# Reordering the opening of a four-layer kernel: row 0 centred before its scale is known, row 1's statistics on ScalarE, the mask pattern stored ahead of the norms

## Chip, cores, metric

One core of a Trainium2 chip runs the whole program. The metric is the device time of one execution in microseconds; the kernel before takes 1152.85 us (median of three runs, 1152.61 to 1153.31). Inputs and outputs are bf16, sums are fp32.

## What is computed

Four layers in the order A, B, A, B, each with a residual: x = x + layer(layernorm(x)). S = 2048 rows, D = 576 columns.

```
def _A_ref(x, wqkv, wo):                 # 32 heads of 18, window 8, dilation 2
    q, k, v = split(x @ wqkv)
    idx = pos[:, None] - 2 * arange(8)[None, :]
    logits = einsum('bhsd,bhswd->bhsw', q, k[idx]) * scale   # -1e9 where idx < 0
    o = einsum('bhsw,bhswd->bhsd', softmax(logits), v[idx])
    return o @ wo

def _B_ref(x, w_in, w_sp, b_sp, w_out):  # gMLP
    z = gelu(x @ w_in); z1, z2 = halves(z)
    g = w_sp @ layernorm(z2) + b_sp
    return (z1 * g) @ w_out
```

Only the opening of the first layer A is changed. What matters of it: layernorm of the input rows, the product of the normalised rows with the v, k and q parts of wqkv, and the mask of the attention window.

## The kernel before

Rows are handled in 16 blocks of 128 ("rows 0" is the first block; even and odd positions are split into the two halves of the sequence, so that a dilation of 2 becomes a window over neighbours). `xnT` holds the normalised rows transposed, 128 x 5 x 2048, and feeds every product on TensorE. Layer A writes v into `v_ext` (17 overlapping tiles of keys, 19 columns for each head, of which the last is 1 and gives the softmax sum), and q and k into `QK`. In `QK` each head takes 32 partitions: 18 of data, 14 "window rows" that hold a mask pattern, so that the product of q and k carries the mask with it.

The opening is written out by hand, in program order on each of the five engines: an instruction waits for its operands and holds everything behind it on its own engine.

- `x_load` fetches row blocks: 0, 1, 2 to 3 apart, then 4 to 7 (into `x1`), 8 to 11 (into the spare part of `oT`), 12 to 15 (`x3`, into the buffer of rows 0 to 3). `load_wv` fetches the v weights, `load_wqk` the q and k weights in six transfers. Nearly all go through SP's queue, one after another.
- 46 matmuls on an identity (line 699) run before there is data; `zero_right` clears the unused halves of three weight tiles on VectorE.
- `build_window_rows` makes the mask pattern and returns four parts. `part0` computes bit patterns on VectorE, `pads` clears the tile `win_pat` on GpSimd, `part1` finishes the pattern in `oT` on VectorE (lines 166 to 173) and stores it to DRAM by two transfers, `part2` makes the pattern of the first eight columns on GpSimd and stores it. `load_pat` fetches the pattern back into `win_pat` by four transfers, spread over partitions. `fill_window_rows` copies it into `QK`: for each half of the head groups (`g0`) one copy for each side (q, k) and a small one of the first columns.
- The layernorm of a block i: `B_` (two bn_stats, line 715), `G_` (bn_aggr, 718), `R_` (add epsilon on VectorE, line 727, then the power -1/2 on GpSimd, 728), `A_` (subtract the mean, times the scale, line 735, into one of four `xn_bufs`). Blocks 0 to 3 are transposed on TensorE (`T_pe`, line 742) and copied by ScalarE into `xnT` (745); blocks 4 to 15 by a transposing transfer on SP's queue (`T_`, line 306).
- `VW(t, hh)` is the product of key tile t with half of the v weights: five matmuls (line 451) into a PSUM bank, evacuated into `v_ext`. Key tile t begins at row 120 t; tile 1 needs the last eight columns of block 0 beside block 1.
- `PG(d, qk, cc)` is the product for q and k: weight block d, 512 columns cc of `xnT`, five matmuls (line 462), evacuated by ScalarE into a staging tile; when a staging tile is full, four or five transfers for each d move the heads into `QK`, by turns on GpSimd's and SP's queues. cc = 0 needs blocks 0 to 3, cc = 1 blocks 4 to 7. After the eighteen units of cc 0 and 1 come `VW` 4 to 7, then cc = 2 and the attention steps.
- Line 703 writes the ones column of `v_ext` on ScalarE; `setup_bufs` clears the pads of the attention's buffers on GpSimd.

PSUM tiles come from a ring of five banks; a tile waits until the bank's former content has been read.

Of the kernel before, what the change touches and what calls it, by code (L numbers as in the profile page):

```python
# [18 lines left out]
P = 128  # L19
# [44 lines left out]
class K:  # L64
# [53 lines left out]
    def build_window_rows(self, c, R):  # L118
# [43 lines left out]
        def pads():  # L162
            nc.gpsimd.memset(pat[:], 0.0)

        def part1(eng):
            nc.vector.tensor_scalar(out=vf[:], in0=bits[:], scalar1=-2.0, scalar2=1.0, op0=ALU.mult, op1=ALU.add)
            Rf = R[:].rearrange("p a r b m -> p a r (b m)")
            nc.vector.tensor_scalar_mul(out=Rf[:, :, 0:8, :], in0=Rf[:, :, 0:8, :], scalar1=vf[:, 4, 1:2])
# [28 lines left out]
    def fill_window_rows(self, QK, half):  # L197
        nc, n = self.nc, self.cfg.S // 2
        for g0 in (0, 4):
            for a in range(2):  # L200
                nc.vector.tensor_copy(out=QK[:, a, g0:g0 + 4, half * n:(half + 1) * n].rearrange("p g (k x) -> p g k x", x=P),
                                      in_=self.pat[:, a, half, None, None, :].to_broadcast([P, 4, n // P, P]))
            if half == 0:
                nc.vector.tensor_copy(out=QK[:, :, g0:g0 + 4, 0:8], in_=self.pat0[:, :, None, :].to_broadcast([P, 2, 4, 8]))
# [176 lines left out]
    def layer_A(self, li):  # L381
# [65 lines left out]
        def VW(t, hh, dve):  # L447
            nk = tdim(t)[0]
            pv = self.PT_tile([P, 512], f32, "pv")
            for c in range(5):  # L450
                nc.tensor.matmul(pv[:nk, 0:288], lhsT=self.xnT[:, c, k0_(t):k0_(t) + nk],  # L451
                                 rhs=wv_sb[:, c, hh * 288:(hh + 1) * 288], start=(c == 0), stop=(c == 4))
            evac(v_ext[:nk, t, 16 * hh:16 * hh + 16, 0:DH], pv[:nk, 0:288].rearrange("p (b d) -> p b d", d=DH), dve)
# [222 lines left out]
        if li == 0:  # L676
# [26 lines left out]
            nc.scalar.copy(out=v_ext[:, :, :, DH:DH + 1], in_=self.ones[:, None, None, :].to_broadcast([P, NT, H, 1]))  # L703
            rows[0]()
            rows[1]()
            setup_bufs(nc.gpsimd)
# [17 lines left out]

            def R_(i0, n):
                rs = rstds[:, i0:i0 + n]
                nc.vector.tensor_scalar_add(out=rs, in0=mvs[:, i0:i0 + n, 1], scalar1=EPS)
                nc.gpsimd.tensor_tensor(out=rs, in0=rs, in1=self.neg_half[:, 0:1].to_broadcast([P, n]), op=ALU.pow)
# [9 lines left out]
            def T_pe(i):  # L738
                xn = xns.pop(i)
# [3 lines left out]
                r = i * P  # L743
                for c0, c1 in ((0, 3), (3, 5)) if i == 0 else ((0, 5),):
                    nc.scalar.copy(out=self.xnT[:, c0:c1, r:r + P], in_=pt[:, c0:c1])  # L745
# [523 lines left out]
```

## Time and profile before

| | |
|---|---|
| median of three runs | 1152.85 us (1152.61 to 1153.31) |
| the profiled execution | 1152.74 us |
| its span, from the first to the last instruction | 1150.9 us |
| TensorE busy in the span | 1142.6 us, 99% |
| VectorE, ScalarE, GpSimd busy | 539.7, 370.5, 259.6 us |
| granted TensorE clock, mean | 1.000 |

How to read the views: a line of the timeline gives the start in us from the span's start, the time, the engine, the source line, the operation, the tiles written and read, a count where equal instructions are merged, and in brackets the idle time of the engine before it and what ended it. An engine with a q (SPq, POOLq) is its sequencer: for a transfer the row is the time to issue it, not to move it. The chain of waits follows the last instruction back, at each step to what released it.

### The profile page before, as it was taken

What the parts mean: (1) busy time and instruction counts of PE and PEld (TensorE: products, weight loads), DVE (VectorE), ACT (ScalarE), POOL (GpSimd) and SP (SyncE); (2) the same over time, 40 slices, a digit from 0 to 9 for tenths busy, and PEclk for the clock granted to TensorE, in tenths of its full rate; (3) what the DMA queues carried; (4) which work ended last, traced back from release to release, by engine and by line L of the source; (5) the groups of instructions that cost most, each with busy time, mean ns of one, the idle gap of its engine ahead of it and who ended that gap; (6) DMA issues with size and microseconds to landing.
All of it is one profiled execution on the core that took longest, in us unless ns stands there. A gap on an engine that the chain in (4) does not pass through costs nothing.

```text
span 1150.9 us, 29693 instructions
## 1 busy us (share of the span) xinstructions
PE 1142.6 (99%) x12930; PEld 614.5 (53%) x12949; DVE 539.7 (47%) x1198; ACT 370.5 (32%) x660; POOL 259.6 (23%) x387
## 2 busy tenths in 40 slices
PE   8999999999999999999999999999999999999998
PEld 5567554444444444457755775544444444444676
DVE  8789987312233222244466889843322223222312
ACT  5589565011111111102247876541111111011000
POOL 3689654000000000002153767530000000000000
PEclk9999999999999999999999999999999999999999
DMA  8877696000000000049455867920000000001322
GB/s 195 183 164 200 141 211 137 10 13 13 13 1 13 13 13 2 1 152 213 110 110 110 180 152 176 246 60 1 13 13 13 13 13 1 13 2 30 101 74 58
DMA packets 177372, 91.26 MB, mean 79 GB/s; under 512 B 128788, under 2 KB 170420, under 8 KB 177242
## 3 DMA queue, kind: packets, MB, share of 16 engines
q1 hardware_dynamic: 164762, 70.75, 28.1%
q0 software_dynamic: 5888, 12.72, 4.6%
q10 hardware_dynamic: 6592, 5.90, 1.7%
q8 instruction: 101, 1.65, 0.6%
q14 instruction: 29, 0.24, 0.1%
HBM read 35.46 MB, written 14.69 MB: 44 GB/s over the span
## 4 chain that ended last, share of the span: by engine, by line
PE 97%; ACT 1%; DVE 1%; issue 0%; DVEq 0%; ACTq 0%
PE hh L234 79%; PE pp L462 6%; PE pv L451 3%; PE pw L629 3%; PE O_ps L559 3%; PE L_ps L536 2%; ACT P_sb L545 1%; PE L_ps L462 1%; PE hh L1191 0%; PE pt L595 0%; DVE ln_st L715 0%; DVE ln_xn L735 0%; DVE win_bits L158 0%; ACT v_ext L445 0%; ACT xnT L745 0%
## 5 line engine op out<-in xcount | busy, mean ns | idle before, releaser
L234 PE MATMUL hh<-Wq,Z 64*128 64x512 bf16 x4608 | 505.8, 376 | 0.0
L234 PEld LDWEIGHTS <-Z 64*128 64x128 bf16 x6984 | 339.8, 94 | 310.1
L1095 DVE TENSOR_TENSOR g_tmp<-hh,ln_xn 128x512 f32<-128x512 f32 x144 | 92.8, 686 | 452.3 <-PE hh L234 452.3
L947 ACT COPY bank_turn<-ones 1x1 bf16<-1x1 bf16 x239 | 44.8, 188 | 538.5 <-PE hh L234 538.5
L78 POOL DMA_DIRECT2D wout<-in_B_w_out_dram x4 | 4.3, 1075 | 602.0 <-PE hh L234 602.0
L234 PE MATMUL hh<-wout,Z 64*128 64x288 bf16 x2232 | 137.0, 283 | 0.0
L545 ACT ACTIVATE P_sb<-L_ps 128x1440 bf16<-128x1440 f32 (+3 forms) x136 | 125.0, 971 | 24.6 <-PE L_ps L536 23.2
L234 PE MATMUL hh<-xnT,w 64*128 64x512 bf16 x1152 | 132.2, 376 | 0.0
L234 PE MATMUL hh<-win2a,xnT 64*128 64x512 bf16 (+1 forms) x960 | 118.7, 355 | 0.0
L234 PEld LDWEIGHTS <-xnT 64*128 64x128 bf16 x1440 | 69.9, 94 | 70.0 <-issue 0.5
L1020 DVE BATCH_NORM_STATS2 z_st<-zp 128x6 f32<-128x512 bf16 (+1 forms) x160 | 93.0, 624 | 13.0 <-ACT zp L1018 12.9
L1086 ACT ACTIVATE z1T<-hh 128x1024 bf16<-128x1024 f32 x72 | 73.7, 1024 | 61.9 <-PE hh L234 61.9
L234 PEld LDWEIGHTS <-w 64*128 64x128 bf16 x1152 | 56.1, 94 | 68.3
L1096 DVE TENSOR_TENSOR Z<-g_tmp,z1T 128x512 bf16<-128x512 f32 x144 | 92.4, 683 | 0.0
L1018 ACT ACTIVATE zp<-hh 128x1024 bf16<-128x1024 f32 (+1 forms) x96 | 76.1, 810 | 48.8 <-PE hh L234 48.6
L462 PE MATMUL pp<-xnT,wqk_sb 128*128 128x512 bf16 (+1 forms) x313 | 74.2, 379 | 0.9
L234 PE MATMUL hh<-win2b,xnT 64*128 64x512 bf16 (+1 forms) x480 | 72.8, 355 | 0.0
L1160 DVE TENSOR_TENSOR x_new<-hh,xo 128x288 bf16<-128x288 f32 x64 | 26.3, 453 | 93.0 <-PE hh L234 85.0
L299 POOL TENSOR_SCALAR ln_xn<-x_new,ln_mv,ln_rstd 128x576 bf16<-128x576 bf16 x28 | 64.2, 2293 | 2.7
L78 POOL DMA_DIRECT2D QK<-stg x76 | 48.0, 636 | 36.5 <-DVE stg L443 21.9
L462 PEld LDWEIGHTS <-wqk_sb 128*128 128x128 bf16 (+1 forms) x360 | 32.1, 97 | 36.6 <-issue 1.9
L1044 POOL TENSOR_SCALAR Z<-zp,z_mv,z_rstd 128x256 bf16<-128x256 bf16 x32 | 50.7, 1584 | 3.5
(124 smaller groups left out, 753.3 us busy)
## 6 DMA issues: line engine op xcount, KB each, us to landing
xres<-x_new SPq DMA_DIRECT2D x44, 144.0 KB
wout<-in_B_w_out_dram POOLq DMA_DIRECT2D x4, 1296.0 KB, 7.4
xo<-xres SPq DMA_DIRECT2D x32, 144.0 KB
xn_rows<-ln_xn SPq DMA_DIRECT2D x28, 160.0 KB
w<-in_B_w_in_dram SPq DMA_DIRECT2D x16, 256.0 KB
QK<-stg POOLq DMA_DIRECT2D x51, 72.0 KB, 4.4
QK<-stg SPq DMA_DIRECT2D x37, 72.0 KB
xo<-in_A_x_dram SPq DMA_DIRECT2D x6, 288.0 KB
```

Source lines behind the costliest of these rows:

```text
L78: return eng.dma_start(out=out, in_=in_)
L234: ins = self.nc.tensor.matmul(outs[a_], lhsT=lhs(a_, c, r0), rhs=rhs(a_, c, r0), start=start and k_ == 0, stop=stop and k_ == len(chunks) ...
L299: e.tensor_scalar(out=xn[:nrows, 0:D], in0=x_t[:nrows, :], scalar1=mv[:nrows, 0:1], scalar2=rstd[:nrows, 0:1], op0=ALU.subtract, op1=ALU.mult)
L462: nc.tensor.matmul(pp, lhsT=w, rhs=self.xnT[r0:r1, c, cc * 512:(cc + 1) * 512], start=start, stop=stop, tile_position=(r0, 0))
L545: nc.scalar.activation(out=P_bufs[2 * jp + s % 2][:nk, :, :, 0:nq], in_=Lv[:nk, :, :, 0:nq], func=ACT.Exp, scale=scale)
L947: self.turn_on = lambda tok: nc.scalar.copy(out=tok, in_=self.ones[0:1, 0:1])
L1018: nc.scalar.activation(out=zp[:, w0:w0 + n], in_=pz, func=ACT.Gelu_apprx_tanh)
L1020: nc.vector.bn_stats(out=st[:, x // 512, :], in_=zp[:, x:x + min(512, w0 + n - x)])
L1044: eng.tensor_scalar(out=Z[:, b0:b1, i, :], in0=zv[:, b0:b1, :], scalar1=mv[:, 0:1], scalar2=rstd[:, 0:1], op0=ALU.subtract, op1=ALU.mult)
L1086: lambda ht, z1T=z1T, q2=q2: nc.scalar.activation(out=z1T[:, q2 * 512:(q2 + 2) * 512], in_=ht[:].rearrange("p a b -> p (a b)"), func=ACT.G ...
L1095: nc.vector.tensor_tensor(out=tmp[:], in0=pg[:, a_, :], in1=bsp[:, qs], op=ALU.add)
L1096: nc.vector.tensor_tensor(out=uT(jj)[:, sub, qs], in0=tmp[:], in1=z1Ts[jj, sub][:, qs], op=ALU.mult)
```

## The change

- Order on SP's queue: the stores of the pattern go behind the load of rows 4 to 7 and ahead of the six loads of the q and k weights; the four loads of the pattern follow these, then rows 8 to 11. Rows 12 to 15 are loaded after the transposes of blocks 4 to 7.
- VectorE: `win_pat` is cleared here; two of the three weight clears go to GpSimd, later; `part1` runs right behind `part0`, ahead of all statistics, with its largest multiplication on GpSimd (line 168). `part2` follows at once, and its store is issued by SP.
- Row block 0: after its mean it is centred without the scale, transposed (`xcT`, in an `o_slot`) and used for `VW(0, 0)` and `VW(0, 1)`; the scale is applied as ScalarE evacuates the product (`scaled`). Block 0 is then normalised and transposed a second time for `xnT`, in two copies (the last eight columns first).
- Row block 1: sum and sum of squares on ScalarE (Identity and Square with an accumulator), mean and scale on GpSimd.
- 35 identity matmuls in place of 46. The ones column of `v_ext` is written in four quarters between the evacuations of the first `PG` units. `setup_bufs` goes behind the scales of blocks 0 to 3.
- `fill_window_rows` is cut in pieces: the first half of the groups between the statistics of block 7 and the normalisation of blocks 6 and 7, the second half around the normalisation of blocks 8 to 11.

```diff
-            nc.gpsimd.memset(pat[:], 0.0)
+            nc.vector.memset(pat[:], 0.0)
...
-            nc.vector.tensor_scalar_mul(out=Rf[:, :, 0:8, :], in0=Rf[:, :, 0:8, :], scalar1=vf[:, 4, 1:2])
+            nc.gpsimd.tensor_scalar(out=Rf[:, :, 0:8, :], in0=Rf[:, :, 0:8, :], scalar1=vf[:, 4, 1:2], scalar2=None,
+                                    op0=ALU.mult)
...
-            x_load(x1[:, 0:4, :], 4, 4, nc.sync)
-            self.load_wqk(nc.sync)
-            x_load(spare, 8, 4, nc.sync)
             exp_table()
-            self.zero_right()
...
-            for _ in range(46):
+            for _ in range(35):
...
-            nc.scalar.copy(out=v_ext[:, :, :, DH:DH + 1], in_=self.ones[:, None, None, :].to_broadcast([P, NT, H, 1]))
+            x_load(x1[:, 0:4, :], 4, 4, nc.sync)
+            rows[1]()
+            nc.vector.memset(wv_sb[64:128, 4, :], 0.0)
             rows[0]()
-            rows[1]()
-            setup_bufs(nc.gpsimd)
+            rows[2](nc.sync)
+            rows[3](nc.sync)
+            self.load_wqk(nc.sync)
+            self.load_pat(nc.sync)
+            x_load(spare, 8, 4, nc.sync)
...
+            def scaled(out, in_):
+                nc.scalar.activation(out=out, in_=in_, func=ACT.Identity, scale=rstds[:, 0:1])
+            sums = sb.tile([P, 2], f32, name="lnx_sum", tag="lnx_sum", bufs=1)
+            spill = self.xn_bufs[1][:, 0:D]
+            nc.scalar.activation(out=spill, in_=xts[1], func=ACT.Identity, accum_out=sums[:, 0:1])
+            nc.gpsimd.tensor_scalar(out=mvs[:, 1, 0:1], in0=sums[:, 0:1], scalar1=1.0 / D, scalar2=None, op0=ALU.mult)
+            nc.scalar.activation(out=spill, in_=xts[1], func=ACT.Square, scale=-1.0, bias=mvs[:, 1, 0:1],
+                                 accum_out=sums[:, 1:2])
             S_(0)
-            R_(0, 1)
-            for i in range(3):
-                B_(i + 1)
-                A_(i)
-                G_(i + 1)
-                R_(i + 1, 1)
-                T_pe(i)
-                for t, hh in (((0, 0),), ((0, 1),), ((1, 0), (1, 1)))[i]:
-                    VW(t, hh, False)
-            rows[2](nc.sync)
+            E_(0, 1)
+            xc = self.xn_bufs[0]
+            nc.vector.tensor_scalar(out=xc[:, 0:D], in0=xts[0], scalar1=mvs[:, 0, 0:1], scalar2=None, op0=ALU.subtract)
+            W_(0, 1)
+            B_(2)
+            pt = T_mm(xc)
+            xcT = o_slots[0]
+            for c0, c1 in ((0, 3), (3, 5)):
+                nc.scalar.copy(out=xcT[:, c0:c1], in_=pt[:, c0:c1])
+            scaled(*VW_mm(0, 0, xcT))
+            A_(0)
+            nc.gpsimd.tensor_scalar(out=rstds[:, 1:2], in0=sums[:, 1:2], scalar1=1.0 / D, scalar2=EPS,
+                                    op0=ALU.mult, op1=ALU.add)
+            W_(1, 1)
+            G_(2)
+            E_(2, 1)
+            A_(1)
+            W_(2, 1)
+            pt0 = T_mm(xns.pop(0))
+            T_out(0, pt0, r0=P - 8)
+            pt = T_mm(xns.pop(1))
+            T_out(1, pt)
+            v01 = VW_mm(0, 1, xcT)
+            scaled(*v01)
+            T_out(0, pt0, r1=P - 8)
+            B_(3)
+            G_(3)
+            E_(3, 1)
+            A_(2)
+            W_(3, 1)
             A_(3)
+            nc.gpsimd.memset(wqk4[64:128, :], 0.0)
+            v0 = VW_mm(1, 0)
+            pt = T_mm(xns.pop(2))
+            T_out(2, pt)
+            evac(*v0, False)
+            v1 = VW_mm(1, 1)
+            pt = T_mm(xns.pop(3))
+            T_out(3, pt)
+            evac(*v1, False)
             VW(2, 0, False)
...
+            setup_bufs(nc.gpsimd)
+            nc.gpsimd.memset(wo_sb[64:128, 4, :], 0.0)
+            S_(4, 5)
+            R_(4, 2)
+            S_(6)
+            A_(4, 5)
+            T_(4, 5)
+            S_(7)
+            R_(6, 2)
+            self.fill_window_rows(QK, 0, (0,))
+            A_(6, 7)
+            T_(6, 7)
             x3 = sb.tile([P, 4, D], bf16, name="x_in3", tag="x_in", bufs=2)
...
-            S_(4, 5)
-            R_(4, 2)
-            A_(4, 5)
-            T_(4, 5)
-            S_(6, 7)
-            R_(6, 2)
-            rows[3](nc.gpsimd)
-            A_(6, 7)
-            T_(6, 7)
-            S_(8)
-            self.load_pat(nc.sync)
-            S_(9, 10, 11)
+            S_(8, 9, 10, 11)
             R_(8, 4)
-            S_(12)
-            A_(8, 9, 10, 11)
-            T_(8, 9, 10, 11)
-            self.fill_window_rows(QK, 0)
-            S_(13, 14, 15)
...
+                if k_ < 4:
+                    hs = slice(8 * k_, 8 * k_ + 8)
+                    nc.scalar.copy(out=v_ext[:, :, hs, DH:DH + 1],
+                                   in_=self.ones[:, None, None, :].to_broadcast([P, NT, 8, 1]))
+                if k_ == 1:
+                    self.fill_window_rows(QK, 0, (4,), (0,))
+                    A_(8, 9, 10, 11)
+                    T_(8, 9, 10, 11)
+                    self.fill_window_rows(QK, 0, (4,), (1,))
+                    S_(12, 13, 14, 15)
```

`T_mm` holds the five transposes of the former `T_pe`, `T_out` its copy on ScalarE; `E_` and `W_` are the two halves of `R_`; `VW_mm` is `VW` without the evacuation.

More of the change, by code (lines that the diff above doesn't have):

```diff
@@ L450, in VW @@
             for c in range(5):
-                nc.tensor.matmul(pv[:nk, 0:288], lhsT=self.xnT[:, c, k0_(t):k0_(t) + nk],
+                nc.tensor.matmul(pv[:nk, 0:288], lhsT=self.xnT[:, c, k0_(t):k0_(t) + nk] if xT is None else xT[:, c, 0:nk],
                                  rhs=wv_sb[:, c, hh * 288:(hh + 1) * 288], start=(c == 0), stop=(c == 4))
-            evac(v_ext[:nk, t, 16 * hh:16 * hh + 16, 0:DH], pv[:nk, 0:288].rearrange("p (b d) -> p b d", d=DH), dve)
+            return v_ext[:nk, t, 16 * hh:16 * hh + 16, 0:DH], pv[:nk, 0:288].rearrange("p (b d) -> p b d", d=DH)
+        def VW(t, hh, dve):
+            evac(*VW_mm(t, hh), dve)
         stg_tiles, stg_left = {}, {}
@@ L742, in T_pe, with T_out @@
                     nc.tensor.transpose(pt[:, c, :], xn[:, c * P:(c + 1) * P], self.ident[:])
-                r = i * P
-                for c0, c1 in ((0, 3), (3, 5)) if i == 0 else ((0, 5),):
-                    nc.scalar.copy(out=self.xnT[:, c0:c1, r:r + P], in_=pt[:, c0:c1])
+                return pt
+            def T_out(i, pt, c0=0, c1=5, r0=0, r1=P):
+                nc.scalar.copy(out=self.xnT[:, c0:c1, i * P + r0:i * P + r1], in_=pt[:, c0:c1, r0:r1])
             def T_(*tiles):
```

24 lines of the change are left out of this document (13 added, 11 removed).

## The prediction

> **What bounds the kernel now.** I read the page's busy times first, then its chain of waits, then that chain and TensorE's waits for the opening alone, then the timeline of the first 30 us.
>
> ```profile
> PE 1142.6 (99%) x12930; PEld 614.5 (53%) x12949; DVE 539.7 (47%) x1198; ACT 370.5 (32%) x660; POOL 259.6 (23%) x387
> ...
> PE 97%; ACT 1%; DVE 1%; issue 0%; DVEq 0%; ACTq 0%
> ```
>
> TensorE sets the time: 1142.6 of 1150.9 us. An edit off TensorE counts only where TensorE waits, so the places where it waits have to be found. The chain of the opening, and TensorE's waits and busy time behind it:
>
> ```profile
> 8.81 0.45 PE pt L742 x5
> ...
> 13.85 10.74 PE pp L462 x49
> ```
>
> ```profile
> PE L_ps L536 <- ACT P_sb L545: 0.2, 1, 0.2
> ```
>
> ```profile
> 13.40:33.00 19.60, 19.50 (x92) 8.91 (x92) 17.47 (x47) 10.38 (x19) 8.03 (x14) 1.00 0.74 141
> 48.00:121.00 73.00, 71.88 (x1422) 50.99 (x1426) 62.86 (x189) 63.59 (x76) 60.59 (x78) 1.00 0.77 184
> ```
>
> Up to 8.81 us the chain runs over VectorE; from there it is TensorE. From 13.42, where the q and k products begin, to 60 us the only wait is 0.2 us on ScalarE; of 13.4 to 33.0 us TensorE is idle for 0.10, of 48 to 121 for 1.12. Nothing that the change moves behind 13.42 us can give back more than these tenths, but it can take. The question is when "pp" (line 462) starts, and whether it then runs without a stop. The steps ahead of it:
>
> ```profile
> 1.10 0.54 DVE L340 MEMSET wqk_sb<- 64x576 uint32 x1 [0.18 <-issue]
> ...
> 1.95 0.30 DVE L342 MEMSET wo_sb<- 64x288 uint32 x1
> ...
> 2.28 0.17 DVE L154 TENSOR_SCALAR win_n<-win_n 128x3 int32<-128x3 int32 x1
> ...
> 3.00 0.98 DVE L158 TENSOR_SCALAR win_bits<-win_g 128x3 int32<-128x3 int32 x4
> ...
> 3.06 0.40 POOL L151 MEMSET ln_xn<- 128x64 bf16 x4
> 3.28 0.70 DVE L160 TENSOR_SCALAR win_bits<-win_n 128x3 int32<-128x3 int32 x1
> 3.39 0.54 POOL L163 MEMSET win_pat<- 128x528 bf16 x1
> 3.56 0.82 DVE L715 BATCH_NORM_STATS2 ln_st<-x_in 128x6 f32<-128x288 bf16 x2
> ...
> 4.42 0.21 DVE L718 BATCH_NORM_AGGREGATE lnx_mv<-ln_st 128x2 f32<-128x12 f32 x1
> ...
> 4.66 0.15 DVE L727 TENSOR_SCALAR lnx_rstd<-lnx_mv 128x1 f32<-128x1 f32 x1
> 4.73 0.81 DVE L715 BATCH_NORM_STATS2 ln_st<-x_in 128x6 f32<-128x288 bf16 x2
> ...
> 5.51 0.43 DVE L735 TENSOR_SCALAR ln_xn<-x_in,lnx_mv,lnx_rstd 128x576 bf16<-128x576 bf16 x1
> ...
> 6.00 0.45 PE L742 MATMUL pt<-ident,ln_xn 128*128 128x128 bf16 x5 [0.65 <-DVE ln_xn L735]
> ...
> 6.49 0.75 ACT L745 COPY xnT<-pt 128x384 bf16<-128x384 bf16 x2 [1.38 <-PE pt L742]
> ...
> 7.03 0.79 PE L451 MATMUL pv<-wv_sb,xnT 128*128 128x288 bf16 x5 [0.57 <-ACT xnT L745]
> ...
> 7.65 0.44 PE L742 MATMUL pt<-ident,ln_xn 128*128 128x128 bf16 x5
> ...
> 7.93 0.78 PE L451 MATMUL pv<-wv_sb,xnT 128*128 128x288 bf16 x5
> ```
>
> From row 0's statistics at s = 3.56 to its transposes at 6.00 take 2.44 us; the first copy on ScalarE, call it a, starts at 6.49 = s + 2.93; pp starts at a + 6.93.
>
> **Row 0 centred first.** bn_stats to bn_aggr 0.86 (3.56 to 4.42), to epsilon 0.24, to the next VectorE instruction 0.07, the centring 0.43 (as line 735), to TensorE 0.06 (5.94 to 6.00): 1.66 in place of 2.44. The first copy then starts at a = s + 1.66 + 0.49 = s + 2.15, a gain of 0.78 us if s stays. It costs a second transposition of row 0 on TensorE: 0.28 us (7.65 to 7.93). A v product takes 0.62 (7.03 to 7.65). TensorE has 8 x 0.62 + 4 x 0.28 = 6.08 us behind the first copy, against 8 x 0.62 + 3 x 0.28 = 5.80; before, the other 1.13 of its 6.93 went to waiting for copies.
>
> I walked ScalarE and TensorE through the new order with intervals from the same stretch (a 128x640 copy 0.60 to the next start, a v evacuation 0.30, the scaled one 0.38 as an estimate). Row 1's copy ends at a + 2.63, so VW(1, 0) starts at a + 2.67 after a wait of 0.33; row 2's copy ends at a + 4.48, just ahead of VW(2, 0); pp starts at a + 7.0. So the second transposition eats what less waiting gives: +0.07 us. VectorE is ahead on this walk: A_(1) at s + 2.95 ends 0.15 before TensorE wants it, A_(2) 0.5.
>
> **The mask pattern ahead of the norms** moves s. Two clears leave VectorE (0.54 and 0.30) and one of about 0.28 enters (264 words, between lines 342 and 340): part0 starts at 1.72 instead of 2.28. But part1 now stands ahead of the statistics:
>
> ```profile
> 8.97 0.16 DVE L166 TENSOR_SCALAR win_vf<-win_bits 128x15 f32<-128x15 int32 x1
> ...
> 9.17 0.28 DVE L168 TENSOR_SCALAR oT<-oT,win_vf 128x256 bf16<-128x256 bf16 x1
> ...
> 9.80 0.25 DVE L173 TENSOR_SCALAR oT<-win_uu 128x4 bf16<-128x4 f32 x2
> ...
> 9.95 0.42 DVE L735 TENSOR_SCALAR ln_xn<-x_in,lnx_mv,lnx_rstd 128x576 bf16<-128x576 bf16 x1
> ```
>
> From line 166 to the next statistic this is 0.98, less 0.21 for line 168: 0.77 us. And it must wait for the bits. These were issued at 3.00 to 3.28 and all ended at 3.98, when GpSimd's run of memsets (line 151, then 163, to 3.93) had ended. Without line 163 that run ends at 3.46, so line 166 starts between 2.98 (bits done as early as they are issued) and 3.50, and s lies at 3.75 or at 4.27 if nothing else interferes. Line 168 on GpSimd is not shown; its nearest rows:
>
> ```profile
> L299 POOL TENSOR_SCALAR ln_xn<-x_new,ln_mv,ln_rstd 128x576 bf16<-128x576 bf16 x28 | 64.2, 2293 | 2.7
> ...
> L179 POOL COPY win_first<-oT 1x224 bf16<-1x224 bf16 x1 | 0.4, 361 | 0.0
> ```
>
> By the copy it takes 0.4 us, by the two-operation scaling 1.0 (256/576 of 2.29), at most 1.6 (halfway from there to the whole 2.29); the copy is nearer, a single pass, and I take 0.6. If VectorE's lines 171 to 173 finish only when it does, as the bits did, s is 3.65 + 0.6 + 0.23 = 4.5, at worst 5.5. I take s = 4.4: row 0's statistics start 0.84 later than now. Then a = 6.55 (6.49 before) and pp starts at 13.55 (13.42 before). The bounds are s = 3.75, pp at 12.9, and s = 5.5, pp at 14.65; row 0's landing, no later than 3.56, gives 12.7 as the floor.
>
> [...]
>
> **Row 1 on ScalarE.** Identity and Square on 576 columns, each at most as long as this row:
>
> ```profile
> L293 ACT ACTIVATE ln_xn<-x_new,ln_nmr,ln_rstd 128x576 bf16<-128x576 bf16 x15 | 13.0, 868 | 62.3 <-POOL bank_turn L1130 59.0 <-POOL ln_nmr L283 3.3
> ```
>
> ScalarE is idle from 2.68 on, as the ones column moves away. But Square waits for a mean from GpSimd, behind line 168 and part2 (an estimate of 0.7: the copy of 0.36, a small one and two memsets; the mean itself 0.25): ready at 3.65 + 0.6 + 0.7 + 0.25 = 5.2, Square ends near 6.0, ahead of a = 6.55. With line 168 at 1.6 us it ends at 7.0, still ahead of that case's a = 7.65. Cost nothing; each 0.1 us beyond is 0.1 us of a.
>
> **Queues.** The two stores, and a third, are put on SP's queue ahead of the q and k weights:
>
> ```profile
> 2.58 2.53 ACT L703 COPY v_ext<-ones 128x544 bf16<-128x544 bf16 x1
> ...
> 4.59 4.50 SPq L78 DMA_DIRECT2D wqk_sb<-in_A_wqkv_dram  x6
> ...
> 10.16 2.24 SPq L78 DMA_DIRECT2D win_period<-oT  x2
> ...
> 14.03 6.20 SPq L306 DMA_TRANSPOSE xnT<-ln_xn  x4
> ...
> 21.81 1.60 SPq L78 DMA_DIRECT2D win_pat<-win_period  x4
> ...
> 24.71 2.36 DVE L201 COPY QK<-win_pat 128x4096 bf16<-128x4096 bf16 x2 [0.39 <-DMA win_pat<-win_period]
> ```
>
> ```profile
> 2.00:4.00 2.00, 2.00 (x22) 2.00 (x20) 1.86 (x11) 1.99 (x3) 1.87 (x16) 1.00 0.96 300
> ```
>
> The weights are issued from about 6.8 instead of 4.59 (stores from 4.6, 2.2 us) to 11.3. From 2 us on the DMA engines are full at 300 GB/s, and rows 0 to 7 with the v weights (1.84 MB) keep them so to about 8.1 us; the weights of the first two pp units (1.25 MB) take 4.2 us from there: 12.3, with 0.5 for the small packets 12.8. They are needed at 13.55 and 14.6. Cost nothing; 0.7 us of slack.
>
> Rows 4 to 7 are needed nine units of 5 x 0.216 us behind the start of pp, at 23.3. VectorE ends A_(3) at 9.65; the statistics of four blocks at 1.0 (3.56 to 4.66 less 0.1 of overlap) and A_(4, 5), 0.7: 14.4. The pattern's four loads, 1.6 us behind the weights, are issued to 12.9 and there by then; two mask copies 2.5: 16.9; A_(6) 0.45; the last two transposes are issued to 20.2, where the four ended before (14.03 + 6.20). Cost nothing; cover: the nine units, some 2 us.
>
> The ones column, four quarters of about 0.7 us, lies in ScalarE's gaps (TensorE gives it 1.08 us for each evacuation of 0.59, and five banks). Starting the moves into QK three microseconds sooner meets no waiting TensorE: worth at most the 0.2 us of the waits above; I count 0.
>
> **The sum.** +0.06 (first copy) + 0.07 (to pp) = +0.13 us on 1152.74, the profiled execution, which stands 0.11 below the median: 1152.9 us.
>
> **Rivals.**
> - *Everything closes.* s = 3.75 (-0.52) or row 0's landing (-0.7), and the later waits go too, since QK is filled sooner: -0.3 to 33 us and around 50, -1.1 up to 121. 1150.6 us at best, 1152 for a third of it; beyond 0.2% only with waits that modelled matmul ends hide. For it: VectorE and GpSimd are idler there. Against it: those waits are on ScalarE's exponentials, which are not touched.
> - *The mask gates rows 4 to 7* (slower). A_(6, 7) now stand behind two copies that wait for the pattern, three transfers deep: stores, weights, loads. It decides once the pattern lands after about 16.5 us; each microsecond later is one of TensorE idle at 23.3. If the loads wait behind the 1.33 MB of weights and rows 8 to 11 as well, landing is near 19: +2.7 us, 1155.5. For it: before, the copies at 24.71 waited for the same transfer, which was issued only at 21.8. Against it: rows 8 to 11 are issued behind it.
> - *TensorE falls back to its slow pace* (slower). 35 warming matmuls end near 4.7, and until 7.1 there is only one transposition.
>
> ```profile
> 1.40:3.80 2.40, 2.40 (x24) 1.00 0.81 237
> 4.20:5.30 1.10, 1.10 (x21) 1.00 1.09 321
> ```
>
> Early identity matmuls come every 100 ns, late ones every 52, though the clock column says 1.00 for both. If the 6.1 us of transposes and v products ran at the slow pace, they would cost up to +6; for half of it +3: 1155.9. It decides from 2.2 us of extra time. Against it: gaps of 0.65 and 0.57 us did nothing before; the new ones are about 1.4 and 0.6. [...]
> - *The change doesn't do what it says*: Square holds the first copy, as priced above; at most +0.5, inside the forecast.
>
> **Chances.** A measurement of this kernel can tell about 0.2% (2.3 us) from no change. Forecast 0.62 (its own range 1152.0 to 1154.0, the bounds of s), everything closes 0.14 (over 0.2% in 0.08), the mask 0.13 (0.10), the pace 0.11 (0.08). Faster 0.08, same 0.74, slower 0.18. The range 1151.0 to 1155.6 leaves out the far halves of three rivals.
>
> **What would show it.** Right: row 0's bn_stats near 4.4, its first ScalarE copy near 6.5, pp at 13.4 to 13.7, no TensorE wait from there to 33 us. [...] A time outside 1150.4 to 1155.2 would mean a wait that I have not seen.

## The result, and the profile after

| | before | after |
|---|---|---|
| median (six runs of each, side by side) | 1153.03 us (1152.61 to 1153.31) | 1158.37 us (1157.67 to 1161.14) |
| ratio | 1 | 1.0050 (95% interval 1.0037 to 1.0063) |
| the profiled execution, its span | 1152.74, 1150.9 us | 1157.67, 1155.9 us |

The change costs 5.3 us, 0.5%. The page of the changed kernel, its busy times and its chain of waits:

```profile
PE 1146.1 (99%) x12943; PEld 615.9 (53%) x12943; DVE 539.8 (47%) x1193; ACT 372.3 (32%) x669; POOL 262.2 (23%) x390
...
PE 97%; ACT 1%; DMA 1%; DVE 1%; issue 0%; POOL 0%; SPq 0%; DVEq 0%; ACTq 0%
```

TensorE is busy 3.5 us longer (1142.6 before), 1.6 of them ahead of the first q and k product (12.17 against 10.54), so part of the loss is slower work, not waiting; and the chain now has 1% on DMA, which it did not have. TensorE's waits from 13.4 to 62 us (line, releaser: us in total, times, longest):

```profile
PE L_ps L540 <- DMA QK<-stg: 1.6, 3, 0.8
PE pp L466 <- DMA xnT<-ln_xn: 0.8, 1, 0.8
```

They have no counterpart before, where the one wait behind 13.4 us was 0.2 us on ScalarE. Where each stands, in TensorE's timeline:

```profile
44.38 0.23 PE L540 MATMUL L_ps<-QK 32*128 32x128 bf16 x3 [0.51 <-DMA QK<-stg]
45.43 0.23 PE L540 MATMUL L_ps<-QK 32*128 32x128 bf16 x3 [0.82 <-DMA QK<-stg]
45.94 0.23 PE L540 MATMUL L_ps<-QK 32*128 32x128 bf16 x2 [0.28 <-DMA QK<-stg]
...
55.39 1.24 PE L466 MATMUL pp<-xnT,wqk_sb 128*128 128x512 bf16 x5 [0.75 <-DMA xnT<-ln_xn]
```

Matmul by matmul against the trace of before, the delay builds up so: +1.43 us at the first q and k product (13.42 to 14.85), +3.60 at the first product with v (48.48 to 52.08; the logits before it arrive in four groups instead of together, which is more than their 1.6 us of waits), +4.38 behind the wait at 55 us, +4.72 at the end of the first feed-forward layer (580.72 to 585.44), +4.57 at the last product, +5.00 at the last instruction. Four places, then: the opening, the attention's start, 0.34 us in the first feed-forward layer, 0.43 us after the last product.

**The opening.** Timeline of the changed kernel:

```profile
3.93 0.96 POOL L168 TENSOR_SCALAR oT<-oT,win_vf 128x256 bf16<-128x256 bf16 x1 [0.43 <-DVE win_uu L170]
...
4.43 0.80 DVE L720 BATCH_NORM_STATS2 ln_st<-x_in 128x6 f32<-128x288 bf16 x2
...
6.02 0.77 ACT L768 ACTIVATE ln_xn<-x_in,lnx_mv 128x576 bf16<-128x576 bf16 x1 [1.40 <-POOL lnx_mv L767]
6.70 0.18 ACT L768 ACTIVATION_READ_ACCUMULATOR ln_xn<-x_in,lnx_mv 128x1 f32 x1
6.79 0.73 ACT L779 COPY o_slot<-pt 128x384 bf16<-128x384 bf16 x2
...
10.35 1.24 DVE L746 TENSOR_SCALAR ln_xn<-x_in,lnx_mv,lnx_rstd 128x576 bf16<-128x576 bf16 x1 [0.44 <-POOL lnx_rstd L735]
10.38 1.05 POOL L802 MEMSET wqk_sb<- 64x1152 bf16 x1
```

Row 0's statistics begin at 4.43. The Square of row 1 waits 1.40 us for its mean, and the first copy can only follow it at 6.79. Row 3's normalisation takes 1.24 us instead of 0.43 while GpSimd's memset runs. The identity matmuls (us, PE busy and their count) and the chain from the first product on:

```profile
1.40:5.40 4.00, 3.88 (x35) 1.00 0.90 258
```

```profile
7.30 1.38 PE pv L452 x5
8.68 1.07 PE pt L752 x10
...
15.01 19.43 PE pp L466 x90
```

All 35 identity matmuls came 0.11 us apart, where before the last 21 came 0.05 apart. From the first v product (five matmuls) to the next start on TensorE the timeline has 1.18 us (7.30 to 8.48) and for the ten transposes behind it 1.06, where before these were 0.62 and 0.56 (the chain counts a piece until the matmul's end, 1.38 and 1.07): TensorE ran at half pace through the first products. The record of the granted clock begins at 9.98 us here and at 4.01 before; ahead of its record the clock column of a view says 1.00, whatever the pace, so "the pace rises" is read below from the start of the record and from the spacing of the matmuls.

**The attention's start.** VectorE and SP's queue in the kernel before:

```profile
17.67 0.81 DVE L715 BATCH_NORM_STATS2 ln_st<-oT 128x6 f32<-128x288 bf16 x2
```

```profile
23.51 5.17 SPq L306 DMA_TRANSPOSE xnT<-ln_xn  x4
28.79 7.71 SPq L78 DMA_DIRECT2D QK<-stg  x9
```

SP's queue in the changed kernel, and VectorE and GpSimd ahead of it:

```profile
6.85 5.06 SPq L78 DMA_DIRECT2D wqk_sb<-in_A_wqkv_dram  x6
12.02 2.27 SPq L78 DMA_DIRECT2D win_pat<-win_period  x4
15.78 0.40 SPq L78 DMA_DIRECT2D oT<-in_A_x_dram  x1
16.27 6.82 SPq L307 DMA_TRANSPOSE xnT<-ln_xn  x4
...
27.32 6.16 SPq L307 DMA_TRANSPOSE xnT<-ln_xn  x4
33.58 7.69 SPq L78 DMA_DIRECT2D QK<-stg  x9
```

```profile
17.22 2.36 DVE L202 COPY QK<-win_pat 128x4096 bf16<-128x4096 bf16 x2 [0.70 <-DMA win_pat<-win_period]
...
20.80 0.81 DVE L720 BATCH_NORM_STATS2 ln_st<-oT 128x6 f32<-128x288 bf16 x2
...
24.92 1.92 POOL L735 TENSOR_TENSOR lnx_rstd<-lnx_rstd,neg_half 128x4 f32<-128x4 f32 x1 [7.62 <-DVE lnx_rstd L731]
...
26.87 1.45 DVE L746 TENSOR_SCALAR ln_xn<-oT,lnx_mv,lnx_rstd 128x576 bf16<-128x576 bf16 x4 [0.90 <-POOL lnx_rstd L735]
```

Rows 8 to 11 are loaded from 15.78, their statistics begin at 20.80 (17.67 before), their transposes are issued from 27.32 (23.51 before), and the seventeen moves into `QK` that share SP's queue start behind them, at 33.58 instead of 28.79. The chain of waits names that as the path, with the wait at 55 us behind it:

```profile
40.49 7.15 DMA QK<-stg
...
52.62 2.63 DMA xnT<-ln_xn
```

**The two small losses.** In the first feed-forward layer ScalarE now waits 0.9 us for TensorE ahead of its table load, where before it loaded at once and waited behind it. At the end SP waits 1.5 us for the last store in one piece (before: 1.1 in two), with seven of the other transfers' semaphores still to be read behind it, which takes 0.43 us (1154.53 to 1154.96), where before the last store's was the last one read:

```profile
ACT L1072 <- PE hh L235: 0.9, 1, 0.9
```

```profile
SPq L1318 <- DMA out_dram<-x_new: 1.5, 1, 1.5
```

### The profile page after: what moved, and what is told of

It is laid out like the page before. It is cut to its first block, busy times and chain, and to the rows that moved or that the text cites. A ratio compares the mean times of both kernels' runs of the same rounds, so it can differ in the third digit from the quotient of the medians.

```text
span 1155.9 us, 29716 instructions
## 1 busy us (share of the span) xinstructions
PE 1146.1 (99%) x12943; PEld 615.9 (53%) x12943; DVE 539.8 (47%) x1193; ACT 372.3 (32%) x669; POOL 262.2 (23%) x390
## 4 chain that ended last, share of the span: by engine, by line
PE 97%; ACT 1%; DMA 1%; DVE 1%; issue 0%; POOL 0%; SPq 0%; DVEq 0%; ACTq 0%
PE hh L235 79%; PE pp L466 5%; PE pv L452 4%; PE pw L633 3%; PE O_ps L563 3%; PE L_ps L540 2%; DMA QK<-stg 1%; PE L_ps L466 1%; ACT P_sb L549 1%; PE hh L1245 0%; DVE QK L202 0%; PE pt L599 0%; DMA xnT<-ln_xn 0%; PE pt L752 0%; ACT L1072 0%
```

## The experiments

Each kernel ran beside the kernel before, whose median was 1153.34 us for the first four, 1152.94 for the next four, then 1152.93 for three, 1152.85, and 1152.94 for the last two. The intervals of the ratios reach 1.0 to 1.5 us to either side, so a difference of 1 us between two changed kernels rests on their traces more than on their times. Theory: the loss is two separate things, the slow pace of the opening and the late blocks 8 to 11.

**46 identity matmuls again, alone** (`range(35)` to `range(46)`).

> The changed kernel with 46 warming matmuls again in place of 35. Theory (the loss is the sum of two: TensorE's slow pace to 10 us, some 1.1 us, and the blocks 8 to 11 that come late for the moves into QK, some 3 us): with 46 the pace rises before the first transposes, the q and k products start at 13.6 (13.3 to 13.9) instead of 14.85, TensorE still waits for the moves at 43 to 46 us and for the transposes at 54 us, and the time is 1.0 to 1.4 us below the changed kernel, about 1157.1. Rival (the pace is not set by the number of warming matmuls, or the products wait for the copies anyway): the start stays at 14.5 or later, as 11 more matmuls at 107 ns end at 6.4 and hold the transposes, and the time is that of the changed kernel or up to 0.6 more.

Measured 1160.38 us, ratio 1.0058 (1.0045 to 1.0071): no gain. The pace rose in time (record from 5.52) and the products started at 14.23, yet TensorE lost it all, and more, to waits for data:

```profile
PE pp L466 <- DMA xnT<-ln_xn: 1.6, 1, 1.6
...
PE pp L466 <- DMA wqk_sb<-in_A_wqkv_dram: 1.1, 1, 1.1
```

Behind the wait of 1.6 us the clock itself was lower. The same execution in two windows (TensorE's busy time is the second number, PEclk the third from the end):

```profile
53.32:56.71 3.39, 1.85 (x37) 0.98 (x35) 2.10 (x5) 2.94 (x4) 1.28 (x3) 1.00 0.92 108
56.73:60.12 3.39, 3.31 (x38) 1.47 (x39) 0.69 (x1) 0.40 (x1) 2.27 (x5) 0.50 1.00 300
```

Behind a stretch in which TensorE was busy 1.85 of 3.39 us the clock is 0.50 for 3.41 us; from 60.14 it is 1.00 again.

**The kernel before with 35** (`range(46)` to `range(35)`).

> The kernel before with 35 warming matmuls in place of 46, nothing else. Theory: fewer of them let the pace rise late here too, the q and k products start at 14.2 to 15 instead of 13.42, the time is 0.7 to 1.5 us above before (1153.7 to 1154.5), and the runs spread wider. Rival (the long gap between warming and the second product is what keeps the pace low, not the count): the pace rises near 4.0 us as before and the time is within 0.3 us of before.

Measured 1153.99 against 1153.34, ratio 1.0003 (0.9994 to 1.0012), runs from 1152.44 to 1155.91. The profiled one (1154.18) had the pace up only at 10.56 and its products from 14.98. So the pace can come late there too. The medians differ by 0.65 us, which the interval does not tell from none; what the other runs did is not seen.

**Mask copies back behind the transposes of blocks 8 to 11, alone; then with 46 matmuls.**

```diff
-            self.fill_window_rows(QK, 0, (0,))
             A_(6, 7)
...
-                    self.fill_window_rows(QK, 0, (4,), (0,))
                     A_(8, 9, 10, 11)
                     T_(8, 9, 10, 11)
-                    self.fill_window_rows(QK, 0, (4,), (1,))
+                    self.fill_window_rows(QK, 0)
```

> The changed kernel with all mask copies put behind the transposes of rows 8 to 11, where they stood before; 35 warming matmuls as changed. Theory: the transposes of rows 8 to 11 are issued from 23.5 to 24.5 instead of 27.3, SP's moves into QK start 3 us sooner, TensorE's waits of 1.6 us at 43 to 46 and 0.75 us at 54 shrink to under 0.5 together; the products still start at 14.85; the time is 2.0 to 2.9 us below the changed kernel, 1155.5 to 1156.4. Rival (the late pattern, the weights' place on the queue or the pow on GpSimd make them late): the transposes are issued at 26.5 or later, and the time is within 0.6 us of the changed kernel.

> Both edits together: 46 warming matmuls, mask copies behind the transposes of rows 8 to 11. Theory of two separate losses: the savings add up, 3.2 to 4.2 us below the changed kernel, 1154.2 to 1155.2; products from 13.6, no wait of TensorE over 0.5 us from 13.6 to 60. Rival (one loss covers the other): the saving is that of the larger one alone, under 3 us.

Measured 1156.75 (1.0031, 1.0021 to 1.0041) and 1156.60 (1.0023, 1.0014 to 1.0033): by the medians about 1.6 us of the 5.3 come from the place of the mask copies, less than expected, and the matmuls add nothing on top. The transposes of blocks 8 to 11 came at 26.50 and 26.78, hardly sooner. The timeline of the second run has the reason:

```profile
16.25 0.40 SPq L78 DMA_DIRECT2D oT<-in_A_x_dram  x1
...
21.15 0.82 DVE L720 BATCH_NORM_STATS2 ln_st<-oT 128x6 f32<-128x288 bf16 x2 [3.08 <-DMA oT<-in_A_x_dram]
```

With the copies gone VectorE stands idle: x rows 8 to 11 are issued only behind the weights and the pattern. In the changed kernel the copies hid this wait. The first of the two runs also shows the clock falling in the opening, to 11.40 us, after 1.49 us of work in 3.39:

```profile
4.58:7.97 3.39, 1.49 (x17) 1.03 (x15) 2.74 (x11) 1.50 (x4) 2.74 (x10) 1.00 1.01 281
7.99:11.39 3.40, 3.40 (x22) 2.52 (x20) 2.89 (x7) 2.28 (x5) 2.10 (x3) 0.50 1.01 107
```

**SP's queue in the earlier order, on top of the last run; and alone.**

```diff
-            rows[2](nc.sync)
-            rows[3](nc.sync)
             self.load_wqk(nc.sync)
-            self.load_pat(nc.sync)
             x_load(spare, 8, 4, nc.sync)
+            rows[2](nc.sync)
+            rows[3](nc.sync)
+            self.load_pat(nc.sync)
```

> The kernel with 46 warming matmuls and the mask copies behind the transposes of rows 8 to 11, and in addition SP's queue in the earlier order: q and k weights, x rows 8 to 11, then the pattern's stores and loads. In the run without this last edit VectorE stood idle for 3.08 us ahead of the statistics of row 8 (21.15), since the load of x rows 8 to 11 was issued only at 16.25. Theory now (that load, behind the pattern's stores and loads, is the second thing that makes the blocks 8 to 11 late, and hid behind the mask copies in the changed kernel): statistics of row 8 at 17.8 to 18.5, transposes of rows 8 to 11 from 23.5 to 24.3, no wait of 0.67 us in the second q and k product and none of 0.9 us at 50 us; the time is 1.8 to 2.6 us below that run's 1156.6, so 1154.0 to 1154.8. Rival (something else holds them, the rows' own statistics or SP's transposes): statistics of row 8 later than 20, time within 0.6 of 1156.6.

> The changed kernel with nothing but SP's queue in the earlier order (weights, x rows 8 to 11, then the pattern's stores and loads); 35 warming matmuls and the mask copies ahead of rows 6 and 7 as changed. Theory (either cause alone makes blocks 8 to 11 late): the statistics of row 8 still begin behind the mask copies, at 20.5 or later, the transposes of rows 8 to 11 from 26.5 or later, and the time is within 0.7 us of the changed kernel's 1158.4. Rival (the queue was the cause all along): transposes from 24.5 or sooner and 1.8 to 2.6 us saved.

On top: 1155.62 (1.0024, 1.0015 to 1.0033), 1.0 us less by the medians, not 1.8 to 2.6; 0.4 of it lies in the kernel before that ran beside each, and the two ratios (1.0023 and 1.0024) show no gain. The trace shows why. The statistics of row 8 began at 17.85 and the waits for weights and moves went, as expected; but a new stop of 1.44 us came at 24.1. The profile puts it down to an evacuation that was done 0.8 us before the stop's end; what was late are the transposes of blocks 4 to 7, behind the pattern's loads, which wait for its stores:

```profile
12.60 0.92 SPq L78 DMA_DIRECT2D win_period<-win_first  x1
16.67 2.04 SPq L78 DMA_DIRECT2D win_pat<-win_period  x4
18.81 5.28 SPq L307 DMA_TRANSPOSE xnT<-ln_xn  x4
```

Alone: 1160.67 (1.0067, 1.0054 to 1.0080), 2.3 us worse than the change as it is, where at most 0.7 was expected. The mask copies stayed ahead of blocks 6 and 7, and with the pattern issued later they gated them:

```profile
19.95 2.36 DVE L202 COPY QK<-win_pat 128x4096 bf16<-128x4096 bf16 x2 [3.57 <-DMA win_pat<-win_period]
```

TensorE's records show a stop of 3.1 us at 24.1. (The pace was up in this execution: record from 5.44, products at 14.24, with the same 35 identity matmuls and the same opening on TensorE as the changed kernel's 9.98 and 14.85.) So the two moves of the change depend on each other: early copies need an early pattern, and the early pattern holds the load of rows 8 to 11.

**TensorE's gap filled; the memset later.** Both on top of the run with 1155.62.

```diff
             pt = T_mm(xc)
+            for _ in range(8):
+                nc.tensor.matmul(warm[:, 0:P], lhsT=self.ident[:], rhs=self.ident[:], start=True, stop=True)
```

```diff
-            nc.gpsimd.memset(wqk4[64:128, :], 0.0)
...
             setup_bufs(nc.gpsimd)
+            nc.gpsimd.memset(wqk4[64:128, :], 0.0)
```

> As the run with 46 warming matmuls, late mask copies and the earlier queue order, with 8 more warming matmuls put between row 0's first transposes and its first product, where TensorE stands idle for 0.66 to 1.0 us. The clock record changes only at the ends of windows of 3.41 us; with TensorE busy for 0.78 of one it rose once and stayed low once, with 0.55 or less it fell. Theory (the pace follows the busy share of such a window, whose place against the kernel's start differs from run to run): with the gap filled the pace rises by 7 us and does not fall, the runs spread by under 1.5 us, and the median lies 0 to 0.6 us below the run without the filling. Rival (the pace is set by the warming block alone): no difference in spread, and up to 0.4 us more, as the matmuls hold the first product.

> As the run with 46 warming matmuls, late mask copies and the earlier queue order, with GpSimd's memset of the weights' last rows (1.05 us from 10.35) put behind its other memsets. It ran beside row 3's normalisation on VectorE, which took 1.24 us instead of 0.43. Theory (the two share a path to memory): row 3's normalisation takes 0.45, its transposes start 0.26 us sooner, and the products start 0.2 to 0.4 us sooner; time 0.2 to 0.4 us lower. Rival (the transposes wait for a copy anyway): normalisation short, start of the products as in the run without it, within 0.1.

Measured 1155.75 (1.0026, 1.0015 to 1.0036) and 1155.64 (1.0024, 1.0015 to 1.0033): no difference. The filled gap tells nothing apart, as the runs without it were close together too, but for one. With the memset later, row 3's normalisation took 0.84 us (other memsets now ran beside it) and the products started at 13.99 instead of 14.23; the stop at 24 us grew from 1.44 to 1.84 in return. What the two engines share was a guess of the theory that no run shows; shown are the scaling's 1.24 us beside the one memset and its 0.84 beside the others. The gain was real and was taken back by the late transposes.

**The pattern's loads behind the transposes of blocks 4 to 7**, on top of the later memset (`self.load_pat(nc.sync)` moved ahead of `S_(8, 9, 10, 11)`).

> The run with 46 warming matmuls, late mask copies, earlier queue order and later memset, and now the pattern's four loads behind the transposes of rows 4 to 7 on SP's queue. In that run the loads waited 2.4 us for the pattern's stores and held these transposes (first at 18.97), so that TensorE stopped for 1.84 us at 23.9. Theory: the first transposes are issued by 15.5, no wait of TensorE over 0.3 us from the start of the q and k products (13.9 to 14.0) to 60 us, and the time falls by 1.4 to 1.8 us to 1153.8 to 1154.3; what is left against before is the later start (0.5), 0.3 in the second layer and 0.4 in the final semaphores. Rival (a new stop takes its place, the moves into QK on SP behind the loads): at most 0.6 us saved.

Measured 1154.49 (1.0014, 1.0005 to 1.0023), 1.15 us less. From the products' start at 13.87 TensorE has no wait left up to 62 us. The two rows are of the opening, ahead of it:

```profile
PE pv L452 <- ACT o_slot L778: 0.8, 1, 0.8
PE pv L452 <- ACT xnT L755: 0.2, 1, 0.2
```

**The pattern finished as before too** (`rows[2]` behind `A_(3)`, `rows[3](nc.gpsimd)` behind `R_(6, 2)`), with 35 and with 46 identity matmuls.

> In addition the pattern is finished where it was before: part 1 behind row 3's normalisation, part 2 and its store on GpSimd behind rows 6 and 7; 35 warming matmuls. What is left of the change is row 0 centred first, row 1's statistics on ScalarE, the ones in quarters and the memsets. Theory (the pattern ahead of the norms cost 0.8 us of start, the centring gains it): row 0's statistics near 3.6, first transposes near 5.3, first copy 5.8 to 6.1, products from 12.8 to 13.3, final semaphores 0.43 us shorter again since the last stores change their place among them; time 1152.2 to 1153.3, level with before or a little under. Rival (the pace stays slow with 35 and gaps): products from 14 or later, 1153.6 to 1154.8.

> The same with 46 warming matmuls. Theory: they end after 6 us where the pace is still low and hold the first transposes by up to 1 us, otherwise they make it rise in time; time within 0.6 us of the run with 35. Rival (35 leave the pace low in most runs): 0.5 to 1.2 us below the run with 35.

Measured 1153.37 (1.0001, 0.9992 to 1.0010) and 1153.54 (1.0008, 0.9999 to 1.0016). With 35, statistics began at 3.51, the first copy at 5.63, the products at 12.85: 0.57 us ahead of before. At the first product with v it was 0.38 us behind (48.86), after a wait for a move into `QK`:

```profile
PE L_ps L540 <- DMA QK<-win2a: 0.3, 1, 0.3
```

SP's moves had started at 28.50, hardly sooner than before, so the earlier TensorE met them.

**The moves sooner**, on top of the run with 35: rows 12 to 15 loaded ahead of the transposes of blocks 4 to 7, the statistics of rows 8 and 12 put into the waits for GpSimd's power.

```diff
+            x_load(x3[:], 12, 4, nc.sync)
             S_(4, 5)
...
             rows[3](nc.gpsimd)
+            S_(8)
             A_(6, 7)
...
-            S_(8, 9, 10, 11)
+            S_(9, 10, 11)
             R_(8, 4)
+            S_(12)
```

> The run with the pattern finished as before and 35 warming matmuls, in which the products started 0.57 us sooner than before and TensorE then lost it again between 41.8 and 48.7 us, waiting for an evacuation on VectorE and for moves into QK. Now the load of x rows 12 to 15 stands ahead of the transposes of rows 4 to 7 on SP's queue, and the statistics of rows 8 and 12 stand in VectorE's waits for GpSimd's pow, so that the transposes of rows 8 to 11 and the moves behind them start sooner. Theory (the moves into QK are what ends that gain): SP's first move at 27.3 to 28.2 instead of 28.5, TensorE's waits between 41 and 49 us under 0.2, the time 0.3 to 0.7 us lower, 1152.6 to 1153.1 and under before's median. Rival (the moves on GpSimd or the evacuations bound it): no change within 0.2 us of 1153.4.

Measured 1152.20 against 1152.85, ratio 0.9996 (0.9987 to 1.0005). SP's moves started at 27.81 and the waits at 41 to 49 us were gone. In this execution, though, the products began only at 14.73, so TensorE came later too; that sooner moves end the wait shows better in the last run below (products at 12.90, moves at 27.71, no wait from there to 62 us, first product with v at 47.96, 0.52 us ahead of before). It is the fastest version by its median, but the interval holds 1: that it beats the kernel before is not shown.

**One store on SP, in the kernel before** (`rows[3](nc.gpsimd)` to `rows[3](nc.sync)`).

> The kernel before with one word changed: the pattern's third store (part 2) is issued on SP's queue and not on GpSimd's, in its old place behind rows 6 and 7. Theory (one more transfer on SP shifts which semaphores the later transfers get, and with them the order of two waits and the place of the last store among the final semaphores): the first feed-forward layer takes 459.67 instead of 459.32 us, from the last product to the last instruction 3.86 instead of 3.43 us, and the time is 0.6 to 1.0 us above before. Rival (these come from other parts of the change): both stay as before and the time is within 0.3 us of before.

Measured 1153.44 against 1152.94, ratio 1.0004 (0.9995 to 1.0013). The end got the 0.43 us (3.86 instead of 3.43 from the last product to the last instruction), with the row of the changed kernel:

```profile
SPq L1264 <- DMA out_dram<-x_new: 1.5, 1, 1.5
```

The feed-forward layer did not (459.33). One half of the theory holds; what makes ScalarE wait ahead of its table load stays open. All kernels here that issue the pattern's stores ahead of the weights or right behind rows 8 to 11 have these 0.34 us, and none of the others.

**The fastest version with TensorE's idle stretches filled** (38 identity matmuls, 6 more behind `T_mm(xc)`).

> The fastest version (row 0 centred, row 1 on ScalarE, pattern as before, moves sooner) with 38 warming matmuls and 6 more between row 0's first transposes and its first product. Its runs fell into two groups, 8 of 11 from 1151.76 to 1152.27 and 3 from 1153.60 to 1154.02; the profiled one, of the second group, got the full clock only at 10.79. Theory (the pace rises at the end of the first window of 3.41 us that is busy enough): with 0.9 or more of every window busy it rises by 7.4 us at the latest, the second group disappears, all runs lie between 1151.7 and 1153.0 and within 1.2 us of each other. Rival (the groups have another cause): some runs at 1153.6 or more, about one in four.

Measured 1153.22, runs spread from 1151.88 to 1155.25: the expectation failed, four of eleven lay above 1153.9. What the profiled executions do show is the size of a late rise. The chains of the two fastest versions, first without the filling (record from 10.79, 1154.02 us), then with it (record from 5.46, 1151.88 us):

```profile
6.64 1.38 PE pv L452 x5
8.02 1.07 PE pt L749 x10
...
14.89 0.22 PE pp L466
```

```profile
6.44 0.80 PE pv L452 x5
...
13.07 19.42 PE pp L466 x90
```

The first q and k products begin at 14.73 and 12.90, 1.8 us apart; the executions end 2.1 us apart. Whether the other runs above 1153.6 are of this kind was not seen, since only one run of each kernel has a trace.

Four times of ten traced executions side by side, with the median of each kernel; "moves" is SP's first into `QK`:

| | products | T of blocks 8 to 11 | moves | first product with v | median us |
|---|---|---|---|---|---|
| before | 13.42 | 23.51 | 28.79 | 48.48 | 1153.03 |
| after | 14.85 | 27.32 | 33.58 | 52.08 | 1158.37 |
| after, 46 matmuls | 14.23 | 28.90 | 34.94 | 52.70 | 1160.38 |
| after, queue back | 14.24 | 30.04 | 36.10 | 56.53 | 1160.67 |
| copies back, 46 | 14.36 | 26.78 | 32.06 | 52.01 | 1156.60 |
| and queue back | 14.23 | 24.82 | 30.09 | 50.88 | 1155.62 |
| and pattern loads last, memset later | 13.87 | 23.07 | 28.41 | 49.28 | 1154.49 |
| pattern as before, 35 | 12.85 | 23.21 | 28.50 | 48.86 | 1153.37 |
| and moves sooner | 14.73 | 22.54 | 27.81 | 49.78 | 1152.20 |
| and idle stretches filled | 12.90 | 22.43 | 27.71 | 47.96 | 1153.22 |

(The trace of "and moves sooner" is of the late pace.) Before, the moves start 15.4 us behind the products and TensorE meets no wait for them. At 15.65 us (pattern as before) it waits 0.3 us, at 17.7 (copies back, 46) 0.9, at 18.7 (after) 1.6: next to nothing was to spare. (With 46 matmuls alone it is 20.7 us and a wait of only 0.5, but there TensorE had been stopped for 1.8 us in between by other waits.)

## Why the prediction was wrong

- **What bounds the kernel** held: behind the start of the products nothing could be gained, only lost, and 2.95 of the 5.0 us were lost there (1.43 to 4.38).
- **The step that failed is "Queues", in its last sentence.** The walk along SP's queue ended at the transposes of blocks 4 to 7 and counted the moves into `QK` as sooner by 3 us, worth 0. They came 4.8 us later, and with the transposes of blocks 12 to 15 behind them they cost the 2.95 us. The walk left out that blocks 8 to 11 stand behind all the moved work (VectorE's copies and the later load), that their transposes stand ahead of the moves on the same queue, and that TensorE's attention waits for those moves with next to nothing to spare. Copies and queue order put back in the right places (with 46 matmuls and the memset later, which gained nothing by themselves) took the time from 1158.4 to 1154.5.
- **Weights, "0.7 us of slack"**: wrong by sign. The walk had the weights of the first two units there at 12.8 us (0.5 of it, for small packets, was the author's estimate, which no run shows); the weights of the second were waited for until 15.81 in the changed kernel and 16.58 with 46 matmuls, where TensorE stopped 1.1 us for them. In the changed kernel the slow pace hid it.
- **Rows 4 to 7, "cost nothing"**: right in the profiled run, with less room than worked out (transposes issued to 23.1, not 20.2). But the pattern was there at 17.2 us (the end of the first copy's wait), not by 12.9, and past the 16.5 at which the rival of the mask gating these rows was to bite. That it did not bite is owed in part to the late products: the nine units end at 24.6 from 14.85, and would have ended at 23.1 from 13.42, just when the last transpose was issued. So "cost nothing" came out partly by luck. The rival did happen, near the predicted place, when the queue alone was put back: 3.1 us at 24.
- **The mask pattern ahead of the norms**: s = 4.4 was 4.43, by luck. The 4.4 had VectorE's lines 171 to 173 end only with line 168 on GpSimd, and line 168 take 0.6 us. It took 0.96, to 4.89, and VectorE did not wait for it: these lines (171 to 174 now) ran beside it from 3.85 to 4.52. What made s late was the start of line 166 at 3.56 (3.50 at most was foreseen) and 0.87 us from there (0.77 foreseen). The scaled evacuation, put at 0.38, took 0.39 to the next start (10.58 to 10.97). "Row 0 centred first": products at a + 7.0 was a + 7.08 where the pace was up and the memset out of the way (6.79 to 13.87). With the pattern as before, the first copy stood at s + 2.12 (3.51 to 5.63; s + 2.15 foreseen) and the products at 12.85: so the centring, together with row 1's statistics on ScalarE, does start the products sooner.
- **Row 1 on ScalarE, "cost nothing"**: 0.24 us. The longer line 168 made the mean later, and each sum takes a separate read of 0.18 us that was not counted; the first copy started at 6.79 instead of 6.55.
- **"TensorE falls back to its slow pace"** had the effect right and the condition wrong: in the changed kernel's trace the pace did not fall back, it had not risen; with the mask copies back, the same opening had it rise at 4.57 and fall back from 7.98 to 11.40. The profiled runs put its price at up to 1.8 us of the products' start. That the 35 matmuls are its cause is not shown: with 35 it also rose at 5.44 and 4.13 (queue back, pattern as before). In the change as it is, putting 46 matmuls back gained nothing, since the data were late.
- **Not seen at all**: 0.34 us at the table load and 0.43 us in the final semaphores, a seventh of the loss.

Shown are the late moves (by the runs that put them back), the mutual dependence of copies and queue order, and the 0.43 us. The cause of the 0.34 us stays open. Only argued is how the 1.43 us of the opening divide between pace (about 0.6, from 14.85 to the 14.23 of runs with the pace up), the memset (0.24) and the rest.

## What to carry to other kernels

Follow a queue that works in order past the first consumer that is safe, down to the last: the transfers behind the moved ones had the smallest slack. Two waits on the same engine can hide each other, so that taking one away shows the next and gains little; put them back together, one by one, until a trace has none. An earlier start of the bounding engine is worth little until the data it meets later come sooner too: here 0.57 us at the first product were gone by the attention's first product with v.

## What the hardware showed

- The granted clock changes in steps of 3.41 us: it was low from 7.98 to 11.40 with the mask copies back, from 56.72 to 60.13 with 46 matmuls alone, and from 49.81 with the queue alone put back, which is one, fifteen and thirteen such steps behind the start of each record (4.57, 5.52, 5.44). The steps lie differently against the start in each execution: with the same opening on TensorE as in two of these runs (4.57 and 5.44) the record of the changed kernel begins at 9.98. The clock fell to 0.50 for one step after TensorE had been busy 1.49 of 3.39 us, 1.85 of 3.39 and 1.73 of 3.38, with no single wait over 1.6 us in the last two. Here half a step of idleness, in pieces, was enough, though not each time: with the memset later TensorE was busy 1.84 of 3.41 us from 24.14, and the clock stayed at 1.00 to 30.90. For the rise, the kernel before was busy 2.65 of the 3.41 us ahead of its record (0.60 to 4.01); the changed kernel was busy 2.67 from 3.16 to 6.57 and stayed slow, and 2.83 from 6.57 to 9.98, where its record begins. Some records of matmuls can be missing, so these shares are rough.
- A VectorE scaling took 1.24 us in place of 0.43 beside a GpSimd memset of 1.05 us, though it starts 0.03 us ahead of it, and 0.84 beside two groups of memsets of 0.41 us each (memset later). GpSimd's power of four columns took 1.92 us beside a VectorE mask copy of 1.22, against 1.03 before. Not every pair is slowed so: in the changed kernel VectorE's lines 171, 172 and 174 ran beside GpSimd's line 168 (3.93 to 4.89) in 0.19, 0.20 and 0.32 us, where before they took 0.19, 0.20 and 0.25. What decides it is not shown.
- One transfer more on SP, 1130 us ahead of the end, came with 0.43 us more at the end (3.86 against 3.43). The trace of the changed kernel, which has the same wait of 1.5 us in one piece, has the last store's semaphore read ahead of seven others, which take those 0.43 us; in the kernel before it is read last (1149.97).
